# A decode block on one core: V's products of a trip's second quarter are moved between its two groups, and 21 constant instructions change engine

## The chip, the cores and the metric

The kernel runs on one core of a Trainium2 chip. The metric is the device time of one execution in microseconds (us); lower is better. TensorE is called PE here, VectorE DVE, ScalarE ACT, GpSimd POOL and SyncE SP, as in the profile.

## What is computed

One token for each of two sequences goes through an attention block and a feed-forward block:

```python
h  = x + softmax(q k^T * 192**-0.5) v @ wo      # q = layernorm(x) @ wq, 32 heads of 192
h2 = h + (gelu(n @ w_gate) * (n @ w_up)) @ w_down   # n = layernorm(h), 640 -> 1536 -> 640
```

Keys and values come from a cache of 8192 positions, of which the last 2048 are used: `k_cache[:, :, 6144:]` and the same of `v_cache`, for 2 sequences of 32 heads, in bf16. Keys and values make up 100 MB of the 122 MB that an execution reads; each byte is used once.

## The kernel before

**Loads.** All large operands pass through one SBUF buffer, `ring`, of three slots of 6 MB. Keys come in eight loads K0 to K7, values in eight loads V0 to V7; load i holds a quarter of the 2048 positions (512 of them) of one sequence, for its 32 heads, so that sequence 0 is i = 0 to 3. K0, K2, K4, K6 use slot 0, K1, K3, K5, K7 slot 1, V0 to V6 slot 2, and V7 slot 0. `load` (line 358) puts a load in a list, and `pump` (361) hands the head of the list to SP's queue once the recorded program has called `done` for what lay in its slot. The order of the list is fixed (lines 437 to 447): wq, K0, K1, V0, K2, V1, K3, V2, K4, V3, K5, V4, K6, V5, K7, V6, V7, wo in four parts, w_gate, w_up, w_down. On the chip SP issues each (line 374) in this order, after waiting for the PE instructions that last read its slot. A V load waits for the products of the V load before it; the K load that stands behind it in SP's queue can't be issued earlier than that V load.

**The loop.** A group g is half a K load, and there are 16. Four trips J = 0 to 3 run over four groups each, so a trip has K loads 2J and 2J+1. For a group the steps are:

- `transposes(g)` (549): 12 times four PE transposes of keys (line 560) into a PSUM bank, copied to `ktr` by DVE (571, seven of them) and ACT (569, five). There are four banks.
- `scores(g)` (613): 24 matmuls (618) from `ktr` and the stationary queries `rq` into the bank `sps`.
- `softmax(g)` (626): DVE adds a mask and takes the maximum (629), ACT takes the exponential (633).
- `e_turn(g)` (656) and `e_blocks(g)` (659): DVE transposes the exponentials and puts them into `eblk`, which has two halves, one for even and one for odd g.
- `pv(g)` (665): 64 matmuls (673) of `eblk` with half a V load, into the bank `ops_` for even g and `m1` for odd g. After the odd one the V load is done. For g % 4 < 2 a DVE copy (683) takes the bank's rows to `osb`.

At a trip's end `maxima`, `sums` (matmul 644) and `combine` (matmuls 687 and 688) work out how the trip's four groups are weighted. `behind(g)` (695) adds the four groups of a trip into `osum`. It stands in the next trip, after that trip's first two groups, and holds `pv` of the earlier trip's last two groups, which is V load 2J-1 in trip J. After every second trip `heads_done` (707) finishes a sequence.

Each engine executes its instructions in the order in which they are recorded, and only PE and DVE run them as a loop. In the second half of a trip (g = 4J+2) the order recorded is:

```python
transposes(g); scores(g); softmax(g)
transposes(g + 1); scores(g + 1); e_turn(g); softmax(g + 1)
maxima(); pv(g - 2); pv(g - 1)
e_blocks(g); e_turn(g + 1); e_blocks(g + 1); sums(); combine()
```

So `pv(g - 2)` and `pv(g - 1)`, the products of V load 2J, stand on PE behind all transposes and scores of K load 2J+1. I call them pv(V 2J), and those in `behind` pv(V 2J-1).

**Constants.** Before the loop POOL and DVE build masks, selections and zeros (lines 450 to 544), while wq and K0 are in flight. POOL also multiplies queries and mask to `rq` (610) at the start and after a trip's last scores.

**The end.** After the loop come `behind(14)` with pv(V7), `heads_done(1)`, `oproj` (727, matmuls 738) over the four parts of wo, the second layernorm and the feed-forward block (from line 809). w_down uses slot 0 and is issued after pv(V7).

Of the kernel before, what the change touches and what calls it, by code (L numbers as in the profile page):

```python
# [7 lines left out]
I32 = mybir.dt.int32  # L8
ALU = mybir.AluOpType
# [7 lines left out]
DH = 192  # L17
# [219 lines left out]
BIG = 1.0e9  # L237
# [9 lines left out]
def bass_sequential_preLN__sliding_block_cached__geglu_ffn__decode_kernel(  # L247
# [12 lines left out]
    with ExitStack() as ctx:  # L260
# [24 lines left out]
        bits = sb("bits", [128, 9], I32)  # L285
        pti = sb("pti", [128, 9], I32)
        pf = sb("pf", [128, 9], F32)
        pg = sb("pg", [128, 14], F32)
        ci = sb("ci", [128, 128], I32)
        cf = sb("cf", [128, 4, 128], F32)  # L290
        ei = sb("ei", [128, 6], I32)
        ef = sb("ef", [128, 6], F32)
        ge = sb("ge", [128, 6, 5], F32)
# [22 lines left out]
        nms = sb("nms", [128, 5], F32)  # L316
        nmin = sb("nmin", [128, 1], F32)
        zr = sb("zr", [128, 5], F32)
# [10 lines left out]
        osb = sb("osb", [128, 2, DH], F32)  # L329
        osum = sb("osum", [128, DH], F32)  # L330
# [7 lines left out]
        hrow = sb("hrow", [128, 320], F32)  # L338
        hsel = sb("hsel", [128, 2, 17], F32)
# [4 lines left out]
        uT = sb("uT", [128, NF, 18], BF16)  # L344
# [4 lines left out]
        ops_ = ps("ops", [128, 512], F32)  # L349
        m1 = ps("m1", [128, 512], F32)  # L350
# [64 lines left out]
        def dve(fn, R=(), W=(), X=(), cls=1):  # L415
            return P.op("dve", fn, R, W, X, cls=cls if looped else 0)
# [7 lines left out]
        def pool(fn, R=(), W=(), X=()):  # L424
            return P.op("pool", fn, R, W, X)

        def ts(out, in0, s1, op0, s2=None, op1=None):
            def fn(e):
                kw_ = {"op1": op1} if op1 is not None else {}
                return e.tensor_scalar(out=out, in0=in0, scalar1=s1, scalar2=s2, op0=op0, **kw_)  # L430
            return fn
# [18 lines left out]
        pool(lambda e: e.iota(ci[:, :], pattern=[[1, 128]], base=0, channel_multiplier=0), W=["ci"])  # L450
        pool(lambda e: e.iota(pi[:, :], pattern=[[0, 1]], base=0, channel_multiplier=1), W=["pi"])
        for k, m in enumerate(BITS):
            pool(lambda e, k=k, m=m: e.memset(bits[:, k:k + 1], m), W=[("bits", k)])
        pool(lambda e: e.iota(ei[:, :], pattern=[[256, 3], [1, 2]], base=0, channel_multiplier=2), W=["ei"])
        pool(lambda e: e.memset(eblk[:, :, :, :, :].rearrange("p a b c d -> p (a b c d)").bitcast(I32), 0), W=[("eb", k) for k in range(2)])

        pool(lambda e: e.memset(uT[:, :, :].rearrange("p a b -> p (a b)").bitcast(I32), 0), W=["uT"])

        P.op("dve", lambda e: e.memset(eps_t[:, :], EPS), W=["eps"], cls=1)
        P.op("dve", lambda e: e.memset(onesd[:, :], 1.0 / D), W=["onesd"], cls=2)  # L460
        dve(lambda e: e.memset(xnT[:, :, :].rearrange("p a b -> p (a b)").bitcast(I32), 0), W=["xnT"])
        dve(lambda e: e.memset(lsx[:, :, :], 0.0), W=["lsx"])
        pool(lambda e: e.memset(hrow[:, :], 0.0), W=["hrow"])
        dve(lambda e: e.memset(sps[:, :], 0.0), X=["s"])
        dve(lambda e: e.memset(m1[:, :], 0.0), X=["m1"])
        dve(lambda e: e.tensor_copy(cf[:, 0, :], ci[:, :]), R=["ci"], W=["cf0"])
# [2 lines left out]
            R=["pi"] + [("bits", k) for k in range(9)], W=["pti"])  # L469
# [51 lines left out]
        pool(ts(selq[:, :], cf[:, 0, 0:32], pg[:, 9:10], ALU.is_equal), R=["cf0", "cqb"], W=["selq"])  # L521
        pool(lambda e: e.tensor_copy(ef[:, :], ei[:, :]), R=["ei"], W=["ef"])
        for r in range(5):
            pool(ts(ge[:, :, r], ef[:, :], 192.0 * r, ALU.is_ge), R=["ef"], W=[("ge", r)])
        pool(tt(mask[:, :, :], ge[:, :, 0:4], ge[:, :, 1:5], ALU.subtract), R=[("ge", r) for r in range(5)], W=["mask"])

        pool(ts(pm[:, :], cf[:, 1, :], pg[:, 4:5], ALU.is_equal), R=["cfm", "p124"], W=["pm"])
        pool(ts(oht[:, :], cf[:, 0, 0:4], rb(3), ALU.is_equal), R=["cf0", "pf"], W=["oht"])
        pool(ts(mska[:, :], cf[:, 1, 0:32], rb(28), ALU.is_equal), R=["cfm", "pf"], W=["mska"])
        pool(ts(mska[:, :], mska[:, :], -1.0, ALU.add, BIG, ALU.mult), R=["mska"], W=["mska"])  # L530
        pool(lambda e: e.memset(nms[:, 4:5], BIG), W=[("nm", 4)])
        pool(lambda e: e.memset(zr[:, 4:5], 0.0), W=[("zr", 4)])
        pool(lambda e: e.memset(osum[:, :], 0.0), W=["osum"])

        def consts_late():
            pool(ts(rowsum[:, :], cf[:, 2, :], 4.0, ALU.mult, pg[:, 4:5], ALU.is_equal), R=["cfm", "p124"], W=["rowsum"])
            pool(ts(rowperm[:, :], cf[:, 3, :], pg[:, 0:1], ALU.is_equal), R=["cfm", "row"], W=["rowperm"])
            pool(ts(mask16[:, :], cf[:, 0, 0:16], pg[:, 5:6], ALU.is_equal), R=["cf0", "p15"], W=["mask16"])
            pool(lambda e: e.iota(cxi, pattern=[[1, 32], [0, 16]], base=0, channel_multiplier=0), W=["cxi"], X=["ktrc"])
            pool(lambda e: e.tensor_copy(cxf, cxi), R=["cxi"], W=["cxf"])  # L540
            pool(ts(colsel[:, :], cxf, rb(31), ALU.is_equal), R=["cxf", "pf"], W=["colsel"] + [("kt", n) for n in range(12)])
            pool(ts(bsel[:, :], cf[:, 0, 0:2], rb(31), ALU.is_equal, 1.0 / D, ALU.mult), R=["cf0", "pf"], W=["bsel"])
            for h in range(2):
                pool(ts(hsel[:, h, :], cf[:, 0, 0:17], 512.0 * h, ALU.add, pg[:, 12:13], ALU.is_equal), R=["cf0", "c63"], W=[("hsel", h)])


        TR = ((0, 0, 0), (2, 0, 1), (1, 0, 0), (0, 1, 1), (1, 1, 0), (2, 1, 0), (2, 2, 1), (0, 2, 0), (1, 2, 1), (0, 3, 0), (2, 3, 1), (1, 3, 0))
# [1 line left out]
        def transposes(g, lo, hi):  # L549

            kk, ktoks = where["k", g // 2]
            kv = kk.bitcast(F32)
            for n in range(lo, hi):
                c, ch, scalar = TR[n]
                bank, x = tps[n % 4], ("t", n % 4)

                def fn(e, c=c, ch=ch, bank=bank):
                    for u in range(4):
                        off = 6144 * (g % 2) + 128 * (3 * (4 * ch + u) + c)
                        ins = e.transpose(bank[:, 128 * u:128 * (u + 1)], kv[:, off:off + 128], identf[:, :])  # L560
                    return ins

                pe(fn, R=ktoks + ["identf"], X=[x])
                if g % 2 == 1 and n == 11:
                    done(("k", g // 2))
                src = bank.bitcast(BF16)
                dst = ktr[:, c, 1024 * ch:1024 * (ch + 1)]
                if scalar:
                    act(lambda e, dst=dst, src=src: e.activation(out=dst, in_=src, func=ACT.Copy), W=[("kt", n)], X=[x])  # L569
                else:  # L570
                    dve(lambda e, dst=dst, src=src: e.tensor_copy(dst, src), W=[("kt", n)], X=[x], cls=0)  # L571
# [54 lines left out]
        def softmax(g):  # L626
            n = g % 4
            dve(lambda e: e.memset(gate[:, :], 0.0), W=["gate"], X=["s"], cls=0)
            dve(lambda e: e.tensor_tensor_reduce(  # L629
                out=sm[:, :].rearrange("p (u x) -> p u x", x=32), in0=sps[:, :].rearrange("p (u x) -> p u x", x=32),  # L630
                in1=mska[:, :].unsqueeze(1).to_broadcast([128, 16, 32]), scale=-1.0, scalar=2.0 * BIG, op0=ALU.add, op1=ALU.min,
                accum_out=nms[:, n:n + 1]), R=["mska"], W=["sm", ("nm", n)], X=["s"], cls=0)
            act(lambda e: e.activation(out=eexp[:, :], in_=sm[:, :], func=ACT.Exp, bias=nms[:, n:n + 1], scale=-1.0,  # L633
                                       accum_out=zr[:, n:n + 1]), R=[("nm", n), "sm", "gate"], W=["eexp", ("zr", n)])
# [30 lines left out]
        def pv(g):  # L665
            vv, vtoks = where["v", g // 2]
            bank, x = ((ops_, "o"), (m1, "m1"))[g % 2]

            def fn(e):
                for a in range(16):  # L670
                    for r in range(4):
                        t = 64 * (g % 2) + 4 * a + r
                        ins = e.matmul(bank[32 * r:32 * (r + 1), 0:DH],  # L673
                                       lhsT=eblk[:, g % 2, a, :, :].rearrange("p s x -> p (s x)")[:, r:128:4],
                                       rhs=vv[:, DH * t:DH * (t + 1)], start=(a == 0), stop=(a == 15),
                                       tile_position=(0, 32 * r), skip_group_check=True)
                return ins

            pe(fn, R=[("eb", g % 2)] + [("eb", g % 2, hg) for hg in range(4)] + vtoks, X=[x])
            if g % 2 == 1:  # L680
                done(("v", g // 2))
            if g % 4 < 2:
                dve(lambda e: e.tensor_copy(osb[:, g % 4, :], bank[:, 0:DH]), W=[("osb", g % 4)], X=[x], cls=0)

        def combine():
            def fn(e):
# [86 lines left out]
        for J in range(4):  # L773
            P.loop_seg("a", J)
            for g in (4 * J, 4 * J + 2):
                transposes(g, 0, 12)
                scores(g)
                softmax(g)
                transposes(g + 1, 0, 12)
                scores(g + 1)  # L780
                e_turn(g)
                softmax(g + 1)
                if g % 4 == 0:
                    if J > 0:
                        P.loop_seg("pa", J)
                        behind(g - 2)
                    if J == 2:
                        P.loop_seg("op", J)
                        heads_done(0)
                    P.loop_seg("a2", J)  # L790
                else:
                    maxima()
                    pv(g - 2)
                    pv(g - 1)
                e_blocks(g)
                e_turn(g + 1)
                e_blocks(g + 1)
                if g % 4 == 0:
                    P.loop_seg("b", J)
                else:  # L800
                    sums()
                    combine()
# [3 lines left out]
        for J in range(4):  # L806
# [3 lines left out]
           R=["rs", "bsel"], X=[("t", 3)])  # L810
# [127 lines left out]
```

## Time and profile before

| what | value |
|---|---|
| median of three runs | 298.16 us (294.39, 298.24, 298.16) |
| the profiled execution, its own time | 294.99 us |
| its span (first to last instruction) | 293.7 us |
| bytes read from HBM | 122.29 MB, 416 GB/s over the span |
| busy: PE, DVE, ACT, POOL | 64%, 50%, 33%, 8% |
| granted PE clock, mean | 0.853 |

The profile is that of one execution. It lists instructions in order of time with their start, their duration and, in square brackets, how long the engine stood idle before and what ended that. "SPq" rows are the moments at which SP issues a transfer; the time from issue to landing is in the answers about a tile. A row of the view by stretches of time gives for each stretch its length, the busy time of the engines asked for, the granted PE clock (1.00 is full), the share of the DMA engines that was busy and the GB/s moved; shares over one only say that a packet's time is booked to the stretch in which it ends.

### The profile page before, as it was taken

How to read it: one execution, taken by the hardware profiler on the slowest of the kernel's cores; microseconds unless marked ns; L12 is line 12 of the kernel's file. 1: busy time of each engine (PE TensorE's matmuls, PEld its weight loads, DVE VectorE, ACT ScalarE, POOL GpSimd, SP SyncE). 2: the span in 40 equal slices, each digit the busy share in tenths (PEclk: the TensorE clock that was granted, in tenths of full speed). 3: DMA queues.
4: the chain of work that ended last, by engine and by line, in shares of the span. 5: the costliest groups of instructions: out<-in, count | busy, mean ns of one | idle time of the engine just before them, and what ended most of it. 6: DMA issues, size and time to landing. Idle time of an engine off the chain costs nothing.

```text
span 293.7 us, 6215 instructions
## 1 busy us (share of the span) xinstructions
PE 188.1 (64%) x2557; PEld 155.5 (53%) x2557; DVE 148.0 (50%) x365; ACT 95.5 (33%) x128; POOL 23.0 (8%) x69
## 2 busy tenths in 40 slices
PE   2007388678848955884788468847881788365385
PEld 1004286476738745763777367637670776352143
DVE  5000036766665673577266746663675266634022
ACT  1001026536506611471266024612650256100001
POOL 8930200000200000002000000020000000000000
PEclk9999959979977996999599959996997599868555
DMA  8999999999889999999999999999999999999994
GB/s 322 486 425 428 424 428 428 424 418 428 353 321 428 428 430 428 428 428 442 442 455 449 428 428 428 428 442 449 428 428 428 428 428 428 428 389 430 423 416 171
DMA packets 4204, 122.46 MB, mean 417 GB/s; under 512 B 478, under 2 KB 608, under 8 KB 1248
## 3 DMA queue, kind: packets, MB, share of 16 engines
q1 hardware_dynamic: 4188, 122.29, 97.0%
q8 instruction: 8, 0.13, 0.2%
q14 instruction: 4, 0.03, 0.0%
q10 hardware_dynamic: 4, 0.00, 0.0%
HBM read 122.29 MB, written 0.00 MB: 416 GB/s over the span
## 4 chain that ended last, share of the span: by engine, by line
DMA 56%; PE 29%; issue 6%; ACT 3%; DVE 3%; SPq 1%; DVEq 0%
DMA ring<-in_A_k_cache_dram 48%; PE tpp L560 19%; DMA ring<-in_A_wo_dram 9%; PE sps L618 3%; PE m L673 2%; PE ops L673 2%; ACT ktr L569 2%; ACT eexp L633 1%; DVE ktr L571 1%; SPq L374 1%; DVE sm L629 1%; PE sps L837 1%; PE m L886 1%; PE m L738 1%; PE ops L837 1%
## 5 line engine op out<-in xcount | busy, mean ns | idle before, releaser
L560 PE MATMUL tpp<-identf,ring 128*128 128x128 f32 x768 | 107.4, 307 | 36.6 <-DMA ring<-in_A_k_cache_dram 30.5
L560 PEld LDWEIGHTS tpp<-identf,ring 128*128 128x128 f32 x768 | 100.1, 160 | 45.6 <-DMA ring<-in_A_k_cache_dram 31.6
L571 DVE COPY ktr<-tpp 128x1024 bf16<-128x1024 bf16 x112 | 77.0, 691 | 54.8 <-PE tpp L560 53.7
L569 ACT ACTIVATE ktr<-tpp 128x1024 bf16<-128x1024 bf16 x80 | 77.4, 1020 | 75.0 <-PE tpp L560 75.0
L618 PE MATMUL sps<-ktr,rq 128*32 128x512 bf16 x384 | 25.2, 390 | 13.7 <-DVE ktr L571 13.7
L633 ACT ACTIVATE eexp<-sm,nms 128x512 bf16<-128x512 f32 x16 | 11.6, 723 | 41.1 <-DVE nms L629 41.1
L618 PEld LDWEIGHTS sps<-ktr,rq 128*32 128x32 bf16 x384 | 10.3, 94 | 24.0 <-ACT ktr L569 17.5
L434 POOL TENSOR_TENSOR rq<-qs,mask 128x192 bf16<-128x192 bf16 x16 | 7.8, 519 | 167.7 <-PE sps L618 154.7
L629 DVE CUSTOM_DVE_ANT_1 sm<-sps,mska 128x512 f32<-128x512 f32 x16 | 11.0, 687 | 16.4 <-issue 16.3
L661 DVE COPY eblk<-et 32x512 bf16<-32x512 bf16 x64 | 18.2, 284 | 2.0 <-DVE nms L629 0.2
L580 PE MATMUL tpp<-ring,xnT 128*32 128x384 bf16 x80 | 5.3, 443 | 15.3 <-DMA ring<-in_A_wq_dram 15.3
L673 PE MATMUL ops<-ring,eblk 128*32 128x192 bf16 x512 | 13.7, 261 | 2.1 <-DMA ring<-in_A_v_cache_dram 2.1
L673 PEld LDWEIGHTS ops<-ring,eblk 128*32 128x32 bf16 x512 | 12.9, 112 | 3.2 <-DMA ring<-in_A_v_cache_dram 2.2
L687 PE MATMUL m<-wz,rowperm 128*128 128x6 f32 x8 | 2.4, 369 | 17.2 <-DVE wz L434 17.2
L673 PE MATMUL m<-ring,eblk 128*32 128x192 bf16 x512 | 12.7, 249 | 0.0
L580 PEld LDWEIGHTS tpp<-ring,xnT 128*32 128x32 bf16 x80 | 2.9, 127 | 17.4 <-issue 15.4
L657 DVE STREAM_TRANSPOSE et<-eexp 128x512 bf16<-128x512 bf16 x16 | 11.3, 706 | 1.0
L673 PEld LDWEIGHTS m<-ring,eblk 128*32 128x32 bf16 x512 | 11.7, 109 | 0.0
L687 PEld LDWEIGHTS m<-wz,rowperm 128*128 128x128 f32 x8 | 2.0, 312 | 17.6 <-DVE wz L434 17.6
L603 DVE CAST qs<-ops 128x384 bf16<-128x384 f32 x1 | 0.6, 557 | 21.3 <-PE ops L598 21.3
L738 PE MATMUL m<-ring,ot 128*2 128x320 bf16 x96 | 6.3, 423 | 6.6 <-DMA ring<-in_A_wo_dram 6.6
L824 ACT ACTIVATE lnv<-tpp,eps_t 98x1 f32<-98x1 f32 x1 | 0.3, 261 | 28.4 <-PE tpp L822 28.4
(144 smaller groups left out, 101.3 us busy)
## 6 DMA issues: line engine op xcount, KB each, us to landing
ring<-in_A_k_cache_dram SPq DMA_DIRECT2D x8, 6144.0 KB, 34.9
ring<-in_A_v_cache_dram SPq DMA_DIRECT2D x8, 6144.0 KB, 22.4
ring<-in_A_wq_dram SPq DMA_DIRECT2D x1, 7680.0 KB, 21.3
ring<-in_A_wo_dram SPq DMA_DIRECT2D x4, 1920.0 KB, 19.2
ring<-in_B_w_gate_dram SPq DMA_DIRECT2D x1, 1536.0 KB, 28.7
ring<-in_B_w_up_dram SPq DMA_DIRECT2D x1, 1536.0 KB, 31.9
ring<-in_B_w_down_dram SPq DMA_DIRECT2D x1, 960.0 KB, 25.5
ring<-in_B_w_down_dram SPq DMA_DIRECT2D x1, 480.0 KB, 26.4
```

The costliest lines, as they stand in the source:

```text
L434: return lambda e: e.tensor_tensor(out=out, in0=a, in1=b, op=op)
L560: ins = e.transpose(bank[:, 128 * u:128 * (u + 1)], kv[:, off:off + 128], identf[:, :])
L569: act(lambda e, dst=dst, src=src: e.activation(out=dst, in_=src, func=ACT.Copy), W=[("kt", n)], X=[x])
L571: dve(lambda e, dst=dst, src=src: e.tensor_copy(dst, src), W=[("kt", n)], X=[x], cls=0)
L580: ins = e.matmul(tps[0][32 * r:32 * (r + 1), 0:384], lhsT=xnT[:, c, 32 * J:32 * (J + 1)], rhs=wq[:, c, 1536 * J + 384 * r:1536 * J + 384 * ...
L618: ins = e.matmul(sps[32 * hg:32 * (hg + 1), :], lhsT=rq[:, k, hg, :], rhs=cols, start=(k == 0), stop=(k == 5), tile_position=(0, 32 * hg))
L629: dve(lambda e: e.tensor_tensor_reduce(out=sm[:, :].rearrange("p (u x) -> p u x", x=32), in0=sps[:, :].rearrange("p (u x) -> p u x", x=32) ...
L633: act(lambda e: e.activation(out=eexp[:, :], in_=sm[:, :], func=ACT.Exp, bias=nms[:, n:n + 1], scale=-1.0, accum_out=zr[:, n:n + 1]), R=[( ...
L657: dve(lambda e: e.transpose(et[:, :], eexp[:, :]), R=["eexp"] + [("eb", 0, 3)] * (g % 2), W=["et"], cls=0)
L661: dve(lambda e, hg=hg: e.tensor_copy(eblk[32 * hg:32 * (hg + 1), g % 2, :, hg, :], et[32 * hg:32 * (hg + 1), :].rearrange("p (a x) -> p a ...
L673: ins = e.matmul(bank[32 * r:32 * (r + 1), 0:DH], lhsT=eblk[:, g % 2, a, :, :].rearrange("p s x -> p (s x)")[:, r:128:4], rhs=vv[:, DH * t ...
L738: ins = e.matmul(m1[32 * r:32 * r + 2, 192:512], lhsT=ot[:, J, kk, :], rhs=wo[:, kk, 320 * h:320 * (h + 1)], start=(J == 0 and kk == 1), s ...
```

## The change

In the second half of a trip the two `pv` are recorded behind `softmax(g)`, ahead of `transposes(g + 1)`. The copies of their results to `osb` become a function of their own, `o_rows`, and stay where they were:

```diff
@@ pv
-            if g % 4 < 2:
-                dve(lambda e: e.tensor_copy(osb[:, g % 4, :], bank[:, 0:DH]), W=[("osb", g % 4)], X=[x], cls=0)
+        def o_rows(g):
+            bank, x = ((ops_, "o"), (m1, "m1"))[g % 2]
+            dve(lambda e: e.tensor_copy(osb[:, g % 4, :], bank[:, 0:DH]), W=[("osb", g % 4)], X=[x], cls=0)
@@ the loop
                 softmax(g)
+                if g % 4 == 2:
+                    pv(g - 2)
+                    pv(g - 1)
                 transposes(g + 1, 0, 12)
...
                     maxima()
-                    pv(g - 2)
-                    pv(g - 1)
+                    o_rows(g - 2)
+                    o_rows(g - 1)
                 e_blocks(g)
```

Before the loop, `pool(` becomes `dve(` for 21 instructions: the nine memsets of `bits` (453), the memsets of `uT` (457), `hrow` (463), `nms`, `zr` and `osum` (531 to 533), the five comparisons into `ge` (524), the two into `hsel` (544), and nothing else:

```diff
         for k, m in enumerate(BITS):
-            pool(lambda e, k=k, m=m: e.memset(bits[:, k:k + 1], m), W=[("bits", k)])
+            dve(lambda e, k=k, m=m: e.memset(bits[:, k:k + 1], m), W=[("bits", k)])
...
         for r in range(5):
-            pool(ts(ge[:, :, r], ef[:, :], 192.0 * r, ALU.is_ge), R=["ef"], W=[("ge", r)])
+            dve(ts(ge[:, :, r], ef[:, :], 192.0 * r, ALU.is_ge), R=["ef"], W=[("ge", r)])
```

In the order that results, PE executes pv(V 2J) behind `scores(4J+2)`, waiting for that V load alone. In SP's queue V load 2J+1 still waits for pv(V 2J); K load 2J+3 behind it now has a wait of its own, for the last transposes of K load 2J+1, and so has the last part of wo.

More of the change, by code (lines that the diff above doesn't have):

```diff
@@ L452, in bass_sequential_preLN__sliding_block_cached__geglu_ffn__decode_kernel @@
         for k, m in enumerate(BITS):
-            pool(lambda e, k=k, m=m: e.memset(bits[:, k:k + 1], m), W=[("bits", k)])
+            dve(lambda e, k=k, m=m: e.memset(bits[:, k:k + 1], m), W=[("bits", k)])
         pool(lambda e: e.iota(ei[:, :], pattern=[[256, 3], [1, 2]], base=0, channel_multiplier=2), W=["ei"])
         pool(lambda e: e.memset(eblk[:, :, :, :, :].rearrange("p a b c d -> p (a b c d)").bitcast(I32), 0), W=[("eb", k) for k in range(2)])
-        pool(lambda e: e.memset(uT[:, :, :].rearrange("p a b -> p (a b)").bitcast(I32), 0), W=["uT"])
+        dve(lambda e: e.memset(uT[:, :, :].rearrange("p a b -> p (a b)").bitcast(I32), 0), W=["uT"])
         P.op("dve", lambda e: e.memset(eps_t[:, :], EPS), W=["eps"], cls=1)
@@ L462, in bass_sequential_preLN__sliding_block_cached__geglu_ffn__decode_kernel @@
         dve(lambda e: e.memset(lsx[:, :, :], 0.0), W=["lsx"])
-        pool(lambda e: e.memset(hrow[:, :], 0.0), W=["hrow"])
+        dve(lambda e: e.memset(hrow[:, :], 0.0), W=["hrow"])
         dve(lambda e: e.memset(sps[:, :], 0.0), X=["s"])
@@ L530, in bass_sequential_preLN__sliding_block_cached__geglu_ffn__decode_kernel @@
         pool(ts(mska[:, :], mska[:, :], -1.0, ALU.add, BIG, ALU.mult), R=["mska"], W=["mska"])
-        pool(lambda e: e.memset(nms[:, 4:5], BIG), W=[("nm", 4)])
-        pool(lambda e: e.memset(zr[:, 4:5], 0.0), W=[("zr", 4)])
-        pool(lambda e: e.memset(osum[:, :], 0.0), W=["osum"])
+        dve(lambda e: e.memset(nms[:, 4:5], BIG), W=[("nm", 4)])
+        dve(lambda e: e.memset(zr[:, 4:5], 0.0), W=[("zr", 4)])
+        dve(lambda e: e.memset(osum[:, :], 0.0), W=["osum"])
         def consts_late():
@@ L543, in consts_late @@
             for h in range(2):
-                pool(ts(hsel[:, h, :], cf[:, 0, 0:17], 512.0 * h, ALU.add, pg[:, 12:13], ALU.is_equal), R=["cf0", "c63"], W=[("hsel", h)])
+                dve(ts(hsel[:, h, :], cf[:, 0, 0:17], 512.0 * h, ALU.add, pg[:, 12:13], ALU.is_equal), R=["cf0", "c63"], W=[("hsel", h)])
         TR = ((0, 0, 0), (2, 0, 1), (1, 0, 0), (0, 1, 1), (1, 1, 0), (2, 1, 0), (2, 2, 1), (0, 2, 0), (1, 2, 1), (0, 3, 0), (2, 3, 1), (1, 3, 0))
```

## The prediction

> **What bounds the kernel now.** I read the DMA part of the profile first, then the stretches of time, then SP's queue, then PE and DVE in order of time.
>
> ```profile
> q1 hardware_dynamic: 4188, 122.29, 97.0%
> HBM read 122.29 MB, written 0.00 MB: 416 GB/s over the span
> ```
>
> The DMA engines are busy for 97% of the span. A gain in the loop has to close a hole in their work, and the stretches show one (busy PE, weight loads, DVE, ACT, POOL, then the PE clock, the DMA share and GB/s):
>
> ```profile
> 76.00:78.00 2.00, 1.14 (x21) 0.60 (x23) 1.31 (x2) 0.87 (x1) 0.00 (x0) 1.00 1.02 442
> 78.00:80.00 2.00, 2.00 (x90) 1.94 (x86) 1.08 (x5) 0.56 (x1) 1.25 (x3) 1.00 0.34 147
> 80.00:82.00 2.00, 1.41 (x63) 1.18 (x52) 0.98 (x4) 0.45 (x3) 0.71 (x2) 1.00 0.03 8
> ```
>
> SP's issues say what was missing:
>
> ```profile
> 54.55 0.54 SPq L374 DMA_DIRECT2D ring<-in_A_k_cache_dram  x1
> 81.34 0.54 SPq L374 DMA_DIRECT2D ring<-in_A_v_cache_dram  x1
> 81.92 0.60 SPq L374 DMA_DIRECT2D ring<-in_A_k_cache_dram  x1
> 107.89 0.54 SPq L374 DMA_DIRECT2D ring<-in_A_v_cache_dram  x1
> 163.19 0.53 SPq L374 DMA_DIRECT2D ring<-in_A_v_cache_dram  x1
> 263.13 4.25 SPq L374 DMA_DIRECT2D ring<-in_B_w_down_dram  x4
> ```
>
> These are K2 (54.55), V1, K3, V2, V4 and w_down. The times to landing of K2, V1 and V2, each from the answer about the tile `ring` on SP in the moment of that issue:
>
> ```profile
> DMA to landing us min/median/max: 27.1/27.1/27.1
> ```
> ```profile
> DMA to landing us min/median/max: 17.5/17.5/17.5
> ```
> ```profile
> DMA to landing us min/median/max: 20.0/20.0/20.0
> ```
>
> K2 lands at 54.55 + 27.1 = 81.65, and only at 81.34 is V1 issued, which lands at 98.84. The distance is 17.2. What a load takes in a full queue, PE's waits give (K3, K4 and K7 begin here):
>
> ```profile
> 113.44 8.01 PE L560 MATMUL tpp<-identf,ring 128*128 128x128 f32 x48 [5.64 <-DMA ring<-in_A_k_cache_dram]
> 142.50 7.16 PE L560 MATMUL tpp<-identf,ring 128*128 128x128 f32 x48 [2.06 <-DMA ring<-in_A_k_cache_dram]
> 229.68 7.92 PE L560 MATMUL tpp<-identf,ring 128*128 128x128 f32 x48 [8.51 <-DMA ring<-in_A_k_cache_dram]
> ```
>
> From K3 to K7 eight loads land in 116.24 us, 14.53 each. So the hole is 17.2 - 14.53 = 2.7 us, and a load has to be issued 17.5 - 14.53 = 3.0 before the one ahead lands, or it tears a hole. V2 is issued 5.5 before K3 lands, V4 8.4 before K5. Those are safe: in every trip but the first, PE waits for K.
>
> **The change, part by part.** First PE and DVE in trip 0, where V1 is released:
>
> ```profile
> 60.64 7.13 PE L560 MATMUL tpp<-identf,ring 128*128 128x128 f32 x48 [3.72 <-issue]
> 68.63 1.51 PE L618 MATMUL sps<-ktr,rq 128*32 128x512 bf16 x24 [0.86 <-DVE ktr L571]
> 70.07 2.40 PE L560 MATMUL tpp<-identf,ring 128*128 128x128 f32 x20
> 77.04 1.61 PE L618 MATMUL sps<-ktr,rq 128*32 128x512 bf16 x24 [0.86 <-DVE ktr L571]
> 78.38 1.52 PE L673 MATMUL ops<-ring,eblk 128*32 128x192 bf16 x62
> 78.71 0.69 DVE L629 CUSTOM_DVE_ANT_1 sm<-sps,mska 128x512 f32<-128x512 f32 x1 [1.18 <-issue]
> 80.03 0.36 DVE L683 COPY osb<-ops 128x192 f32<-128x192 f32 x1 [0.16 <-PE ops L673]
> 81.35 0.36 DVE L683 COPY osb<-m 128x192 f32<-128x192 f32 x1 [0.96 <-PE m L673]
> 85.72 0.59 PE L687 MATMUL m<-wz,rowperm 128*128 128x6 f32 x2 [4.31 <-DVE wz L434]
> 86.59 7.78 PE L560 MATMUL tpp<-identf,ring 128*128 128x128 f32 x48
> ```
>
> Today pv(V0) begins 1.34 behind the start of the second scores and V1 is issued 2.96 after that. Moved, it begins at 68.63 + 1.34 = 69.97, if V0 is there. V0 was issued ahead of K2, lands by one load before it, 81.65 - 14.53 = 67.1, and is. V1 goes out at 69.97 + 2.96 = 72.93, 8.7 before K2 lands: **this hole is closed**, worth at most 2.7.
>
> What is moved past what: K3, behind V1 on SP, keeps a wait for the second transposes. These now begin at 72.83 and take about 6.8 to their scores (6.97 today with softmax on DVE in between, which pv now covers), so K3 goes out near 79, long before V1 lands at 96.2: nothing. The results stay in two banks until the copies behind `maxima`; their next writer is the pv in `behind`, over 20 us later: nothing. The DVE copies find their banks ready, and the waits of 0.16 and 0.96 go. POOL's multiplication of the next queries follows the later scores, ahead of a first use some 15 us off: nothing.
>
> **What is late next is V2.** PE does the same work, but now the whole of group 3 lies behind pv. The path from the release of V1 to that of V2:
>
> - second scores at 72.83 + 6.8 = 79.6; mask on DVE 1.67 later (77.04 to 78.71)
> - from there to line 687: 7.01 today (78.71 to 85.72), less 1.12 of waits, is 5.89: 87.2
> - to K2's transposes 0.87: 88.1, against 86.59 today
> - through two groups and pv(V1) to V2's issue 21.30 (86.59 to 107.89): 109.35.
>
> K3 now lands at 81.65 + 2 x 14.53 = 110.7. V2 is issued only 1.4 before it, where 3.0 are needed, so a new hole of 1.6 opens. V2 lands at 109.35 + 17.5 = 126.9 instead of 127.9. **Of 2.7, 1.0 is left.**
>
> **The later trips** get a wait that they did not have: V 2J follows K 2J+1 in the queue by 14.53, but PE asks for it some 10 us after that K. PE stands about 5 us in mid-trip and goes on with a slow clock. The nearest rows are those of V7, whose pv waited too:
>
> ```profile
> 258.75 2.76 PE L673 MATMUL ops<-ring,eblk 128*32 128x192 bf16 x64 [2.14 <-DMA ring<-in_A_v_cache_dram]
> ```
>
> w_down, which pv(V7) releases, was issued at 263.13: 4.38 after the landing, against 2.96 warm. With L the landing of V2 (or V4) the next release falls at L + 4.38 + 6.8 + 1.67 + 5.89 + 0.87 + 21.30 = L + 40.9. It has to be there 3.0 before the third landing after L, at L + 43.6 - 3.0 = L + 40.6. So each of two trips loses 0.3: V4 and V6 come with 0.7 and 0.4 of the gain left. The ends of 21.30 are that and 20.69 (142.50 to 163.19, where PE was waiting for K4), with which there is no loss; I take the longer, since PE will not be waiting for K.
>
> **The end** follows V6: wo stands behind V7 in the queue. pv(V7) starts near L + 18.7 + 0.9 with L at V6 (243.7), so at 263.3, and ends at 267.7; `heads_done` takes 3.6 (263.1 to 266.67 today), three slow quarters of wo 1.77 each, so PE is ready for the last quarter at 276.6:
>
> ```profile
> 266.67 0.29 PE L733 MATMUL m<-xrow,identb 2*2 2x320 bf16 x2 [1.07 <-DVE ot L724]
> 278.02 1.77 PE L738 MATMUL m<-ring,ot 128*2 128x320 bf16 x24 [2.74 <-DMA ring<-in_A_wo_dram]
> ```
>
> That lands at 278.0 - 0.4, so the loads still decide, with 1 us to spare.
>
> **The constants.** 21 instructions leave POOL, about 3 us of it.
>
> ```profile
> 7.89 0.20 DVE L434 TENSOR_TENSOR xnT<-dT,lt 128x40 bf16<-128x40 f32 x1 [1.27 <-ACT lt L490]
> 7.95 1.03 POOL L430 TENSOR_SCALAR ge<-ef 128x6 f32<-128x6 f32 x5
> 16.30 0.77 POOL L430 TENSOR_SCALAR hsel<-cf,pg 128x17 f32<-128x17 f32 x2
> 22.58 5.28 PE L580 MATMUL tpp<-ring,xnT 128*32 128x384 bf16 x80 [15.32 <-DMA ring<-in_A_wq_dram]
> 29.41 0.56 DVE L603 CAST qs<-ops 128x384 bf16<-128x384 f32 x1 [21.32 <-PE ops L598]
> ```
>
> xnT is ready at 8.1 and wanted at 22.58, when wq lands; a DVE front longer by about 1 us is covered 14 times. From 8.1 to 29.41 DVE is idle, and takes the rest. POOL waits for `ge` from DVE, and ends before 17 as today. Price zero; without the cover it would be those 3 us.
>
> **Sum.** 294.99 - 2.7 + 1.7 + 2 x 0.3 = 294.6, against the profiled execution's own 294.99. That run stands 3.2 below the median of the three shown (298.16), of which one was at 294.39 and two near 298.2; the loads' order does not say which of the two the next will take, so the range holds both.
>
> [...] A load's price beyond its bytes is 3.0 here. [...]
>
> **The rivals.**
>
> *The full gain.* V2 goes out by 107.7, before K3's landing needs it; the path from 69.97 to 109.35 would have to be 1.6 shorter. For it: no softmax between the transposes, and later trips pass their two groups 0.6 faster. Against it: the other steps are rows as they stand. 294.99 - 2.7 = 292.3.
>
> *PE's loop becomes the bound* (slower). The place is the wait for V 2J in mid-trip. If the slow clock outlasts pv, the second transposes suffer too.
>
> ```profile
> 112.00:113.00 1.00, 0.00 (x0) 0.50 1.71 737
> 113.00:114.00 1.00, 0.56 (x3) 0.50 0.11 49
> 117.00:118.00 1.00, 1.00 (x7) 0.50 1.25 541
> 118.00:119.00 1.00, 1.00 (x8) 0.73 0.57 246
> ```
>
> Here the clock (third number from the right) stayed at 0.50 for 5 us after work resumed at 113.44, and the first transposes took 8.9 to their scores instead of 6.8. With 2.1 more a trip loses 2.4: 294.99 - 1.0 + 2 x 2.4, and 1.1 at the end beyond the slack of 1, is 299.9. It decides from about 0.5 us more per trip than I took. [...]
>
> *The change does nothing*: DVE's new constants or V0 itself come late. V0's landing has 2.9 us in hand, the constants 14. Time 295.0 or, without the constants' cover, 298.
>
> **Chances.** Forecast, within 1.5 of 294.6: 0.50. Full gain: 0.20. PE's loop: 0.25, of which a third beyond 2%. Nothing: 0.05. A measurement of this kernel tells about 2% from no change, 5.9 us: faster than 289.1 is out of reach of a hole of 2.7 (0.02); slower than 300.9 has 0.08; within 0.90. Range: from the full gain less the 0.6 by which the fastest run shown was quicker, 291.7, to the slow rival, 300.0, which also holds no change at the upper of the runs' two levels.
>
> **What would show it.** Right: V1 issued near 73; no weak stretch at 78 to 82 but one near 110; PE waiting about 5 us for V in lines 673 of trips 1 to 3; V2, V4 and V6 issued near 109, 168 and 226. Wrong: V2 issued before 107.7 (full gain) or V4 after 169 (the loop bounds); a PE start on K0 later than before (the constants).

## The result, and the profile after

The change makes the kernel slower by about 1%: the ratio to the kernel before is 1.012, with an interval of 1.0094 to 1.0146. The medians of 22 runs are 301.10 us (296.50 to 305.81) and 294.38 us (292.44 to 298.24); their ratio, 1.023, is higher than 1.012 because that compares only the runs within 1.5% of the fastest of each kernel. The profiled execution took 298.69 us, of which 297.3 are its span, against 294.99 and 293.7. So 3.6 us have to be found in the trace; the median execution, 2.4 us longer than the profiled one, lost more than that.

The DMA part of the changed kernel's page, which stood at 97.0% and 416 GB/s:

```profile
q1 hardware_dynamic: 4188, 122.29, 96.3%
HBM read 122.29 MB, written 0.00 MB: 411 GB/s over the span
```

The bytes are the same, and the queue stands idle for longer. The view by stretches (busy PE, weight loads, DVE, ACT, POOL, then PE clock, DMA share, GB/s) shows where:

```profile
78.00:80.00 2.00, 2.00 (x15) 2.00 (x14) 0.84 (x2) 0.68 (x1) 0.00 (x0) 0.66 0.78 295
80.00:82.00 2.00, 2.00 (x21) 1.96 (x20) 1.82 (x3) 1.65 (x3) 0.00 (x0) 1.00 1.17 393
108.00:110.00 2.00, 1.14 (x15) 0.74 (x17) 1.78 (x3) 1.43 (x2) 0.00 (x0) 1.00 0.63 270
110.00:112.00 2.00, 2.00 (x74) 1.53 (x68) 0.90 (x5) 0.07 (x1) 0.00 (x0) 1.00 0.01 4
112.00:114.00 2.00, 2.00 (x91) 1.85 (x80) 1.55 (x5) 0.74 (x2) 0.00 (x0) 1.00 0.00 0
114.00:116.00 2.00, 1.67 (x16) 1.43 (x14) 1.77 (x6) 1.17 (x2) 0.00 (x0) 1.00 1.19 393
```

The old hole at 80 to 82 (8 GB/s) is gone but for a short weak stretch (98 GB/s from 82 to 83). A new one stands at 110 to 115, with nothing moved for some 5 us. SP's issues in the changed kernel name the load that was late:

```profile
53.83 0.54 SPq L374 DMA_DIRECT2D ring<-in_A_k_cache_dram  x1
77.42 0.54 SPq L374 DMA_DIRECT2D ring<-in_A_v_cache_dram  x1
83.86 0.54 SPq L374 DMA_DIRECT2D ring<-in_A_k_cache_dram  x1
113.87 0.53 SPq L374 DMA_DIRECT2D ring<-in_A_v_cache_dram  x1
171.45 0.54 SPq L374 DMA_DIRECT2D ring<-in_A_v_cache_dram  x1
```

These are K2, V1, K3, V2 and V4. The answers about `ring` at the issues of K3 and of V2:

```profile
DMA to landing us min/median/max: 27.8/27.8/27.8
```
```profile
DMA to landing us min/median/max: 17.4/17.4/17.4
```

K3 lands at 83.86 + 27.8 = 111.66, V2 is issued 2.2 us after that, at 113.87, and lands at 131.27: 19.6 behind K3, 5.1 more than the 14.53 of a full queue. ("Lead" below is the time by which a load is issued before the landing of the load ahead of it; V2's is -2.2.) Why V1 and V2 were issued so late, PE's order of time tells:

```profile
60.48 8.07 PE L560 MATMUL tpp<-identf,ring 128*128 128x128 f32 x48 [4.28 <-issue]
69.40 1.61 PE L618 MATMUL sps<-ktr,rq 128*32 128x512 bf16 x24 [0.86 <-DVE ktr L571]
70.73 1.52 PE L673 MATMUL ops<-ring,eblk 128*32 128x192 bf16 x62
72.13 1.26 PE L673 MATMUL m<-ring,eblk 128*32 128x192 bf16 x47
76.56 0.83 PE L673 MATMUL m<-ring,eblk 128*32 128x192 bf16 x15 [3.16 <-issue]
77.32 6.51 PE L560 MATMUL tpp<-identf,ring 128*128 128x128 f32 x48
92.31 0.59 PE L688 MATMUL m<-wz,rowperm 128*128 128x6 f32 x2 [4.58 <-DVE wz L434]
131.35 2.75 PE L673 MATMUL ops<-ring,eblk 128*32 128x192 bf16 x64 [6.81 <-DMA ring<-in_A_v_cache_dram]
133.89 1.53 PE L673 MATMUL m<-ring,eblk 128*32 128x192 bf16 x64
190.32 1.52 PE L673 MATMUL ops<-ring,eblk 128*32 128x192 bf16 x64 [2.06 <-DMA ring<-in_A_v_cache_dram]
248.45 1.52 PE L673 MATMUL ops<-ring,eblk 128*32 128x192 bf16 x64 [3.70 <-DMA ring<-in_A_v_cache_dram]
```

The moved products start at 70.73 as they should, run 47 instructions into their second bank, and then PE stands for 3.16 us with "issue" as the releaser: nothing that the profile shows held it. That stop is not in the trace of before. Further down are the new waits for V in mid-trip.

The budget of the 3.6 us, by the landings of the V loads (issue plus time to landing; where PE waits, its row with "<-DMA ring" begins within 0.1 us of that):

| landing | before | change | behind | by itself |
|---|---|---|---|---|
| V2 | 127.9 | 131.3 | 3.4 | hole at V2 5.1, V1 itself 1.0 over 14.53, less the old hole of 2.7 |
| V4 | 186.1 | 190.25 | 4.15 | 0.8 in the second trip |
| V6 | 244.15 | 248.4 | 4.2 | 0.1 |
| end of span | 293.7 | 297.3 | 3.6 | 0.6 given back behind V6 |

### The profile page after: what moved, and what is told of

It reads as the page before. It is cut to its first block, busy times and chain, and to the rows that moved or that the text cites. A ratio compares the mean times of both kernels' runs of the same rounds, so it can differ in the third digit from the quotient of the medians.

```text
span 297.3 us, 6207 instructions
## 1 busy us (share of the span) xinstructions
PE 187.7 (63%) x2557; PEld 154.6 (52%) x2557; DVE 148.6 (50%) x386; ACT 96.0 (32%) x128; POOL 20.1 (7%) x48
## 4 chain that ended last, share of the span: by engine, by line
DMA 38%; PE 38%; issue 12%; DVE 8%; ACT 2%; SPq 1%; DVEq 0%
PE tpp L560 25%; DMA ring<-in_A_v_cache_dram 19%; DMA ring<-in_A_k_cache_dram 12%; DMA ring<-in_B_w_down_dram 8%; PE ops L673 5%; PE m L673 4%; PE sps L618 3%; DVE eblk L661 2%; DVE et L657 2%; DVE ktr L571 1%; ACT ktr L569 1%; ACT eexp L633 1%; DVE osb L684 1%; PE m L688 1%; PE m L689 1%
## 5 line engine op out<-in xcount | busy, mean ns | idle before, releaser
L560 PE MATMUL tpp<-identf,ring 128*128 128x128 f32 x768 | 105.5, 304 | 22.3 <-DMA ring<-in_A_k_cache_dram 11.0
L560 PEld LDWEIGHTS tpp<-identf,ring 128*128 128x128 f32 x768 | 99.1, 159 | 29.6 <-DMA ring<-in_A_k_cache_dram 11.7
L673 PE MATMUL ops<-ring,eblk 128*32 128x192 bf16 x512 | 14.7, 276 | 12.6 <-DMA ring<-in_A_v_cache_dram 12.6
L661 DVE COPY eblk<-et 32x512 bf16<-32x512 bf16 x64 | 18.5, 288 | 1.8
L673 PE MATMUL m<-ring,eblk 128*32 128x192 bf16 x512 | 13.7, 261 | 3.2 <-issue 3.2
L580 PE MATMUL tpp<-ring,xnT 128*32 128x384 bf16 x80 | 6.1, 494 | 15.3 <-DMA ring<-in_A_wq_dram 15.3
L673 PEld LDWEIGHTS m<-ring,eblk 128*32 128x32 bf16 x512 | 12.4, 113 | 3.4 <-issue 3.4
L587 ACT ACTIVATE qrow<-tpp 128x768 bf16<-128x768 f32 x1 | 0.8, 812 | 20.8 <-PE tpp L580 20.8
```

Of the source, the lines that this page charges most:

```text
L580: ins = e.matmul(tps[0][32 * r:32 * (r + 1), 0:384], lhsT=xnT[:, c, 32 * J:32 * (J + 1)], rhs=wq[:, c, 1536 * J + 384 * r:1536 * J + 384 * ...
L661: dve(lambda e, hg=hg: e.tensor_copy(eblk[32 * hg:32 * (hg + 1), g % 2, :, hg, :], et[32 * hg:32 * (hg + 1), :].rearrange("p (a x) -> p a ...
L673: ins = e.matmul(bank[32 * r:32 * (r + 1), 0:DH], lhsT=eblk[:, g % 2, a, :, :].rearrange("p s x -> p (s x)")[:, r:128:4], rhs=vv[:, DH * t ...
```

## The experiments

In all of them the ratio is to the kernel before, timed beside it on the same chip. Two theories stand at the start: that the order makes V2's issue late (through PE's stop, the granted clock of 0.50 after it from 76 to 79, and the whole second group now lying behind pv), or that the constants do it.

**The order alone, and the constants alone.** The first keeps the 21 instructions on POOL and moves pv; the second is the reverse.

```diff
-                if g % 4 == 2:
-                    pv(g - 2)
-                    pv(g - 1)
...
+                    pv(g - 2)
                     o_rows(g - 2)
+                    pv(g - 1)
                     o_rows(g - 1)
```

(This is the constants alone, as an edit of the changed kernel.)

> Only the products of V load 2J are moved; all 21 constants stay on POOL. Theory A: the loss is the order's, because V2 is released later on PE (a stop of about 3 us inside the moved products in trip 0, where their code is executed for the first time, and then the whole second group behind them). By A the ratio to the kernel before is that of the full change, 1.009 to 1.015, V2 is issued near 113 to 114, and a hole in the transfers opens just behind 110. Theory B: the constants on DVE cost it. By B the ratio is 0.99 to 1.00 and V2 goes out near 109.

> Only the 21 constants move to DVE; the products stay at the trip's end. Theory A: same as the kernel before, ratio 0.998 to 1.002, V1 issued near 81, V2 near 108. Theory B: ratio 1.009 to 1.015.

Measured: the order alone 1.0226 (1.016 to 1.0292), median 302.07; the constants alone 0.9988 (0.9961 to 1.0015), median 294.27. The order costs all of it. Its ratio lies above the expected 1.009 to 1.015, a miss; its median, though, is close to the change's 301.10. PE and SP in the order alone:

```profile
72.79 1.27 PE L673 MATMUL m<-ring,eblk 128*32 128x192 bf16 x49
76.43 0.53 PE L673 MATMUL m<-ring,eblk 128*32 128x192 bf16 x15 [2.36 <-issue]
```
```profile
114.39 0.53 SPq L374 DMA_DIRECT2D ring<-in_A_v_cache_dram  x1
172.21 0.54 SPq L374 DMA_DIRECT2D ring<-in_A_v_cache_dram  x1
```

The stop is there again, with the same 15 products left behind it, so it belongs to a place in the program. V2, V4 and V6 land at 131.9, 191.9 and 252.7: here the distances are 60.0 and 60.8, against 58.1 (4 x 14.53) in a full queue, so this execution, of 304.04 us, lost 1.9 and 2.7 us in its later trips, where the change's own profile lost 0.8 and 0.1.

**Halves of K and V, in both orders.** If late issue is the whole cause, then the orders must come out alike where the queue is always issued ahead. Each 6 MB load is cut into two, and each half's place in the ring is given back by itself.

```diff
-            load(("k", i), K_AT[i % 2], SLOT, kv_src(A_k_cache, i), lambda v: v, f"k{i % 2}")
+            for h in range(2):
+                load(("k", i, h), K_AT[i % 2] + h * SLOT // 2, SLOT // 2, kv_src(A_k_cache, i)[:, :, 12288 * h:12288 * (h + 1)],
+                     lambda v: v, f"k{i % 2}{h}")
...
-                if g % 2 == 1 and n == 11:
-                    done(("k", g // 2))
+                if n == 11:
+                    done(("k", g // 2, g % 2))
```

(The same for V, at lines 388, 666 to 681.)

> The kernel before with every K and V load cut into two loads of 3 MB, each with its own release; order and constants as before. If a late V1 is the kernel's only hole (2.7 us) and a hole opens just where a V load is issued less than 3 us before the load ahead lands, this version has none: PE starts 6 us earlier on K0, V1 is issued near 74 with K2 landing at 81.7. Expected 292.3 against 295, ratio 0.991. If instead each transfer has a price of its own that a full queue does not hide, 16 more transfers make it slower than the kernel before.

> The full change with every K and V load cut into two of 3 MB. Theory A: PE has 6 us more in trip 0, which is more than the 4.5 us by which V2 came late, so no hole opens; ratio to the kernel before 0.991 to 0.995, about as the old order with halves. Theory C, by which the waits for V in mid-trip and the slow clock behind them make PE's loop the bound: the ratio stays over 1.005, since every trip still waits for V load 2J in its middle.

Measured: 0.9944 (0.9926 to 0.9963), median 293.12, in the old order; 0.9939 (0.9913 to 0.9965), median 293.36, in the new one. The orders are alike. In the old order the gain is smaller than the 0.991 that was expected. The new order with halves, GB/s in 40 slices of its span, and then PE's waits in mid-trip:

```profile
GB/s 324 446 416 431 427 429 427 427 427 430 431 431 429 431 429 418 431 431 435 431 431 428 428 431 431 431 431 431 431 431 431 431 431 431 422 428 423 423 414 165
```
```profile
60.16 1.52 PE L677 MATMUL ops<-ring,eblk 128*32 128x192 bf16 x64 [1.98 <-DMA ring<-in_A_v_cache_dram]
67.48 2.76 PE L677 MATMUL m<-ring,eblk 128*32 128x192 bf16 x64 [5.79 <-DMA ring<-in_A_v_cache_dram]
```

No slice between the first and the last is under 414: no hole. PE still waits for V in mid-trip, here by 5.79 us, and the bank of products behind that wait still takes 2.76 us, where the one ahead of it took 1.52, and none of it reaches the end. In this kernel a wait in mid-trip costs time only through the release that stands behind it.

**What the stop is.** In the trace of before and of the change, a packet on an instruction queue ends in the same stretch, 74 to 75 (from the DMA view of that stretch, before and then the change). The view names neither the queue's engine nor what the packet holds, and no run here shows that it is PE's code; what follows shows only where and when the stop comes.

```profile
q8 instruction: 1, 0.02, 6.2%
```
```profile
q8 instruction: 1, 0.02, 6.0%
```

In the change the packet's 0.02 MB are booked at 74.3, and PE goes on at 76.56, 2.3 us later. The stop stands behind the 185th matmul of the trip's second half, which the new order reaches at 73.4. The old order reaches the 180th only at about 79, when the packet of 74 to 75 has ended, and shows no stop. Its trace with the constants alone was a little earlier, and shows a shorter stop behind the 180th, with a packet in 75 to 76 (the halves of V in the old order show one of 0.62 us at the same place):

```profile
76.48 0.99 PE L673 MATMUL ops<-ring,eblk 128*32 128x192 bf16 x36
78.39 0.78 PE L673 MATMUL ops<-ring,eblk 128*32 128x192 bf16 x28 [0.93 <-issue]
```

To test whether the place belongs to the code, 40 tiny matmuls whose result is not used stand ahead of `q_rows` in the changed kernel, so that all later code is 40 products further on:

```diff
+        def pad(n):
+            def fn(e):
+                for k in range(n):
+                    ins = e.matmul(m2[:, 48:50], lhsT=xrow[0:2, 0:D:NC5], rhs=identb[0:2, 0:2], start=True, stop=True)
+                return ins
+
+            pe(fn, R=["xrow", "identb"], X=["m2"])
+
+        pad(40)
```

> The full change, with 40 tiny matmuls more on PE before wq lands, where PE stands idle for 14 us anyway; their result is not used. They shift all later PE code by 80 instructions. In the two traces of the new order PE stopped at the same instruction (47 and 49 matmuls into the second of the moved products) while one packet of instructions landed. Theory A1: that stop is a code fetch that the short moved products outran; shifted, the fetches fall where PE runs slower, the stop of 3 us goes, V1 is issued near 74 and V2 near 111, and the ratio to the kernel before falls to 1.000 to 1.006. Theory A2: the stop does not matter, since only the serial path from the second group to V2 counts; then the ratio stays at 1.010 to 1.02.

Measured: 1.0139 (1.0054 to 1.0225), median 299.19. PE:

```profile
70.12 0.45 PE L673 MATMUL m<-ring,eblk 128*32 128x192 bf16 x9
74.79 2.12 PE L673 MATMUL m<-ring,eblk 128*32 128x192 bf16 x55 [4.23 <-issue]
```

55 products are left behind the stop instead of 15: it moved by exactly 40. So it stands at a fixed place in the code; the packet is in 72 to 73 here (at 72.4), and PE goes on 2.4 us later. That the stop would go was a miss: it is 4.23, longer than before, as PE comes to the place 2.8 us sooner and goes on only 1.8 sooner. V1 and V2 were issued at 76.94 and 113.22, not near 74 and 111. The ratio lies in the range of theory A2, but since the stop stayed, this run does not tell what the stop costs, and does not speak for A2.

**Halves of K alone, halves of V alone, and the change once more.** Each half of the edit above by itself in the new order, with the unchanged change beside them.

> The full change with only the K loads cut in two; V loads stay whole. If the hole at V2 is closed by PE's earlier start on K0 and K1, this has nearly the whole effect of cutting both: ratio 0.993 to 0.997. If it is V's earlier release, it stays above 1.005.

> The full change with only the V loads cut in two. The first half of V2 is released 1.3 us earlier than the whole, and that is all that is won in trip 0; the hole of about 5 us at V2 shrinks by 1.3, and those at V4 and V6 go. Ratio 1.003 to 1.010. If the release of V decides instead of PE's start, 0.993 to 0.997.

> The full change once more, on the chip of these runs, as their base. Ratio 1.010 to 1.022 (the two measurements of the new order so far were 1.012 and 1.023); a stop inside the second moved product in trip 0, V2 issued near 114, and the weak stretch in the transfers behind 110.

Measured: K alone 1.0062 (1.003 to 1.0093), median 296.66, where less than 1 was expected, a miss; V alone 1.0038 (0.9994 to 1.0082), median 295.40, as expected; the change 1.0093 (1.0058 to 1.0128), median 297.96, just under the expected range. The second trace of the change, an execution of 296.98 us, is the most telling of all; V2, expected near 114, went out at 110.36. PE and SP:

```profile
57.50 1.97 PE L560 MATMUL tpp<-identf,ring 128*128 128x128 f32 x16 [1.26 <-issue]
68.96 1.24 PE L673 MATMUL m<-ring,eblk 128*32 128x192 bf16 x49
72.95 0.83 PE L673 MATMUL m<-ring,eblk 128*32 128x192 bf16 x15 [2.76 <-issue]
128.10 2.76 PE L673 MATMUL ops<-ring,eblk 128*32 128x192 bf16 x64 [7.13 <-DMA ring<-in_A_v_cache_dram]
130.64 2.78 PE L673 MATMUL m<-ring,eblk 128*32 128x192 bf16 x64
```
```profile
110.36 0.54 SPq L374 DMA_DIRECT2D ring<-in_A_v_cache_dram  x1
170.50 0.54 SPq L374 DMA_DIRECT2D ring<-in_A_v_cache_dram  x1
226.57 1.18 SPq L374 DMA_DIRECT2D ring<-in_A_v_cache_dram  x2
```

PE lost only 1.26 us at the start of the second half where the profile above shows 4.28, and was 3 us earlier all along. V2 landed at 128.1, as in the kernel before. The old hole at V1 was gone, and one of 2.4 us at V2 took its place. But behind the wait for V2 both banks of products were slow (2.76 and 2.78 us, where the first trip's first bank took 1.52), V4 was issued 1.2 us ahead of K5's landing, landed at 188.0, 59.9 behind V2, and 1.9 us were gone. The span is 295.6, those 1.9 above before. So a later trip loses time by itself, even where the first has lost none.

The halves divide the loss between the trips. With halves of K the first trip has neither the stop nor a hole (V2 lands at 126.0, 14.5 behind the load ahead), but V4 was issued only at 167.71, 41.7 behind V2's landing, with a lead of 2.0, and lost 1.4; V6's release was 39.7 behind V4's landing and lost nothing. With halves of V the stop is there (3.45 us), the first half of V2 was issued 0.3 behind K3's landing and lost 3.3, and V4 and V6 lost nothing.

**The same halves in the old order.** If only the loads' head start mattered, the old order would gain as little from them.

> The kernel before with only the V loads cut in two. In the old order the one hole is V1's, 2.7 us; its first half is released about 1.3 us earlier, so half of the hole goes: ratio 0.994 to 0.997.

> The kernel before with only the K loads cut in two. PE starts 6 us earlier on K0, V1 is released before it is needed, the hole goes whole: ratio 0.990 to 0.995. It then differs from the new order with K halves (1.006) only in the order, with PE's head start in both; if head start were all that counts, the two would be alike.

Measured: V alone 0.9969 (0.994 to 0.9997), median 294.47; K alone 0.9915 (0.9891 to 0.994), median 292.30, the fastest kernel of the study, 0.85% faster than before. Both ratios are in the expected ranges. For halves of V the mechanism is not shown: its traced execution was a long one (297.66 us), in which V1's first half went out 1.1 behind K2's landing. The page of halves of K:

```profile
q1 hardware_dynamic: 5340, 122.30, 98.1%
```

With the same head start the old order gains 0.85% and the new one loses 0.6%. The difference is put down to the path from one V's landing to the next V's release: in the old order PE's waits stand at K instead, and V4 is issued 11.7 us ahead, against 2.0.

**That path made shorter.** With half of the score products left out (the scores are then sums over half of a head's columns), a trip's path on PE is shorter; this is done in the change and in the change with halves of K.

```diff
-                for k in range(6):
+                for k in range(3):
...
-                                       stop=(k == 5), tile_position=(0, 32 * hg))
+                                       stop=(k == 2), tile_position=(0, 32 * hg))
```

> The full change with the K loads cut in two, and with the second half of the score products left out (12 of 24 matmuls of each group, so the scores are sums over half of the head's columns). This takes about 0.7 us of PE per group, 2.8 per trip, from the path between a V landing in mid-trip and the release of the V load after next. Theory C for the later trips (that path of 40 to 42 us leaves no time before the K load ahead has landed): the holes at V4 and V6 go and the ratio falls from 1.006 to 0.992 to 0.997. If the later trips lose by something else, such as the price of cutting the loads, it stays above 1.003.

> The full change with whole loads and with the same half of the score products left out. Four groups lie ahead of V2's release, which comes 2.5 to 3 us earlier than in the full change, and the later trips gain 2.8 each: ratio 0.997 to 1.005 against 1.009 to 1.012, with what is left due to the stop for code in trip 0, which is not touched. If PE's path were not what delays V2, the ratio would not fall.

Measured: 0.9975 (0.9949 to 1.0002), median 293.87, with halves of K, where the same with all scores was 1.0062; 1.0001 (0.9968 to 1.0034), median 294.30, in the change, where it was 1.0093. The first is just above its expected range, the second in it. In the change this also takes 48 products out of a trip, which moves the stop into the second transposes:

```profile
76.72 3.30 PE L560 MATMUL tpp<-identf,ring 128*128 128x128 f32 x28 [1.89 <-issue]
```

There V1 was issued at 72.53 and V2 at 108.01. So in this run two causes are lessened at once, the path and the place of the stop; what each is worth alone it does not tell. The halves of K do tell the path's part, since their first trip shows no stop, with all scores or with half. The issue of V4, with all scores and then with half:

```profile
167.71 0.53 SPq L374 DMA_DIRECT2D ring<-in_A_v_cache_dram  x1
```
```profile
165.95 0.53 SPq L374 DMA_DIRECT2D ring<-in_A_v_cache_dram  x1
```

That is 41.7 and 39.0 behind V2's landing, the lead grows from 2.0 to 4.8, and V4's loss falls from 1.4 to 0.2. So the fall from 1.0062 to 0.9975 is the shorter path's. What is left there is a hole of 1.1 at V2 (lead 3.7). In the change with half of the scores, too, V4 and V6 lose nothing; their releases are 38.7 behind the landings.

## Why the prediction was wrong

The forecast was 294.6, no change that can be measured. It came out 1.2% slower, and the median of the changed kernel, 301.1, lies above the range.

**The step that failed** is "V1 goes out at 69.97 + 2.96 = 72.93". pv began at 70.73, 0.76 later, as the granted clock stayed at 0.50 in the transposes ahead of it until about 65.7, against 63.9 before; from there to the issue of V1 it took 6.69 us, not 2.96. Of the 3.73 between them 3.16 are the stop, and the rest is the clock of 0.50 behind it. The 2.96 came from a stretch without a stop. Moved, the products of the first trip came to that place at 73.4, ahead of the packet at 74.3, and stood for 3.16 us here, and for 2.36, 2.76, 3.45 and 4.23 in four other traces. Where the stop fell elsewhere, with the half scores, V1 went out at 72.53.

V2 was to go out 1.4 ahead of K3's landing and went out 2.2 behind it, so its hole is 5.1 instead of 1.7. Of the 4.1 us by which the profiled execution lies above the forecast (298.69 against 294.6), 3.4 are this hole, 1.0 is V1, which also landed late, 0.3 the later trips, less 0.6 at the end. The rest of the path to V2's issue, forecast 109.35 and measured 113.87, held up:

| part of the path | forecast | measured | difference |
|---|---|---|---|
| start of pv | 69.97 | 70.73 | 0.76 |
| pv to V1's issue | 2.96 | 6.69 | 3.73 |
| second transposes to scores | 6.8 | 7.37 | 0.57 |
| scores to line 688 (687 before) | 7.56 | 7.62 | 0.06 |
| to K2's transposes | 0.87 | 0.88 | 0.01 |
| two groups and pv to V2's issue | 21.30 | 20.68 | -0.62 |

**The second failed step** is a size, "a load has to be issued 3.0 before the one ahead lands, or it tears a hole". It came from one hole, V1's, and holds only for loads issued as late as that. These are all whole V loads of the traces with a lead up to 5.1 us:

| lead | loads | issue to landing | landing behind the load ahead, over 14.53 |
|---|---|---|---|
| -3.3 to 2.0 | 9 | 17.4 to 17.9 | 6.3 falling to 1.4: 2.9 to 3.4 less the lead |
| 2.2 to 4.2 | 6 | 18.5 to 19.7 | 0.7 to 2.7 |
| 4.4 to 5.1 | 10 | 18.9 to 19.9 | at most 0.25 |

In the middle row a need of 3.0 would leave at most 0.8. So no hole at all takes a lead of about 4.4 us, and below that the loss does not grow evenly as the lead shrinks: it was 2.7 at 2.2 and both 0.7 and 1.9 at about 3.3, but 1.8 at 1.2. Why, no run here shows. The 3.0 of late loads has its shape in one-us stretches of the changed kernel around V2 (busy PE, clock, DMA share, GB/s):

```profile
109.00:110.00 1.00, 0.39 (x8) 1.00 0.46 197
110.00:111.00 1.00, 1.00 (x26) 1.00 0.02 8
114.00:115.00 1.00, 1.00 (x12) 1.00 0.00 0
115.00:116.00 1.00, 0.67 (x7) 1.00 2.37 786
```

K3's last data came near 110.0 and its landing was signalled at 111.66, 1.7 later; V2 was issued at 113.87 and its packets begin to end after 115, at least 1.1 later. Together that is about 2.9, as is the hole of 5.1 less the 2.2.

**The later trips.** The release of the next V was forecast at 40.9 behind a landing; it came at 40.2 and 39.1 in the change, 40.3 and 41.4 in the order alone, 42.4 and 38.6 in the second trace of the change. That is 40.3 on the mean, so the path was about right. But with a lead of 4.4 it is due at 43.6 - 4.4 = 39.2 or earlier, not at 40.6. So the new order has nothing to spare in any trip, and the traces lose between 0 and 2.7 us in each. Slow products make part of the difference. The second trace released V4 2.2 us later behind the landing than the first: 1.2 of this are the two banks of products behind the wait for V2, 5.25 us from the first of them to the next transposes (128.10 to 133.35) instead of 4.00 (131.35 to 135.35); the other 1.0 lies behind them. That fits the spread of the changed kernel's runs, 9 us, where the three kernels without a hole at V spread by 0.2 (halves, old order), 0.7 (halves, new order) and 0.3 (halves of K, old order), though with 4 to 10 runs each.

The slow rival named the right place, the wait for V in mid-trip, and a time of 299.9. Its own step, second transposes that take 8.9 to their scores, did not come: behind waits of 6.81 and 7.13 they took 6.4 and 6.7. By the table most of the profiled execution's loss came through the stop, which no rival had; that 299.9 lies near the measured times is largely luck.

**What was right.** The hole at V1 closed but for 1.0; V2 was late next, with the weak stretch near 110; PE waits for V in mid-trip (6.81 in the first); the constants cost nothing (0.9988); the end did not take the bound (0.6 given back behind V6).

**What stays open.** What the stop waits for, why its length varies between 2.4 and 4.2 us, and what sets when the packet ahead of its end comes. Whether V1's 1.0 is a matter of its lead of 4.2: with the half scores V1 came 0.6 late with a lead of 9.0. What the change would take without the stop and with nothing else altered was not isolated; the second trace of the change bounds it from one side, as its first trip lost nothing against before and its later ones still 1.9.

## What to carry to other kernels

When a step is moved so that it releases a buffer earlier, work out the next release on the same path as well: what was behind the step is now ahead of the next one, and a queue that had 8 us in hand in every trip may have none. Take the lead that a load needs from the distances between landings at several leads, not from one hole: here one hole gave 3.0, and the queue kept full only from 4.4 on. And look at the first pass of a loop by itself: here a short step that came sooner stood there for 2.4 to 4.2 us, with "issue" as the releaser, and in the change in no later pass; smaller loads with a release of their own (292.3 us for halves of K in the old order) did here what the reordering was not able to do.

## What the runs showed of the hardware

PE stopped in a straight run of instructions, with "issue" as the releaser. In the new order with all scores the stop of 2.4 to 4.2 us stood at a fixed place in the code, moved by 40 products with the code, and ended 2.3 to 2.5 us behind a packet of 0.02 MB on an instruction queue (76.56 behind 74.3 in the change, 76.43 behind 74.1 in the order alone, 74.79 behind 72.4 with the shifted code, 72.95 behind 70.5 in the second trace of the change). In the change it was absent from the later trips, and of the eight packets (0.13 MB) of that queue none falls between 90 and 262 us. That PE waits there for its own code was not shown. PE also stood with "issue" as the releaser at the start of the second half of trip 0, where it passes over `behind`, which that trip leaves out (3.72, 4.28 and 1.26 in the rows at 60.64, 60.48 and 57.50).

The pace after a wait was not the same from trace to trace. Behind waits of 6.81 us in the change and 7.13 in its second trace the first bank of products took 2.75 and 2.76 us, the second 1.53 in the one and 2.78 in the other. In the change the granted clock stood at 0.50 for 2.6 us after work resumed at 131.35; in the second trace the two slow banks take the 5.3 us from 128.10 to 133.42. The forecast had taken the slow time to end with pv.
